# A plan's costs for transfers and TensorE transposes, and its table of priorities, replaced in an attention and two-MoE kernel

## The chip, the cores and the metric

The kernel runs on one core of one Trainium2 chip. The metric is the device time of one execution in microseconds (us): the median of several runs. A profiled execution of its own gives the trace that is read here.

## The reference, cut to what matters

The program computes attention with a window of 32 keys (heads 0 to 3 plain, heads 4 to 7 with every fourth position), and puts its output through two feed-forward blocks.

```python
B, H, S, D = 4, 8, 576, 64
scores = where(mask[h], q @ k.T / sqrt(D), -1e9)        # mask: 32 positions back, plain or dilated by 4
x = (softmax(scores) @ v).transpose(0, 2, 1, 3).reshape(B, S, 512)

x_prev = shift_by_one_position(x)
xk = mu_k * x + (1 - mu_k) * x_prev                     # 512 wide
xr = mu_r * x + (1 - mu_r) * x_prev
kk = relu(xk @ w_k)                                     # w_k 512 x 1024
x = sigmoid(xr @ w_r) * (kk * kk @ w_v)                 # w_r 512 x 512, w_v 1024 x 512

h = relu(x @ w_in); u, vv = halves(h)                   # w_in 512 x 1024
vs = einsum('ts,bsd->btd', w_spatial, layernorm(vv)) + b_spatial
out = (u * vs) @ w_out                                  # w_out 512 x 512
```

## The kernel before, in words

Every product in float32 is made of matmuls on numbers split into a high and a low part (names that end in h and l, or chunk numbers that end in _0 and _1), three matmuls for one product: high by high, high by low, low by high. Batch 0 to 3 follow one another; each batch has two halves of 320 and 256 positions in the first feed-forward block.

The weights w_k, w_r and w_v come in chunks of 128 rows by 512 columns (CH), one transfer of 128x1024 32-bit words each, since a number of the input fills two words. `split_weight` turns a chunk into numbers: the chunk lands in one of four places of the tiles room2 and room3 (`raws`), ScalarE makes two passes over it (temps<-room and room<-room), VectorE joins them (SCALAR_TENSOR_TENSOR temps<-temps,room), and then `split` makes the high part (a CAST or copy, on ScalarE or on VectorE) and the low part (TENSOR_TENSOR, number minus high part, on GpSimd or on VectorE). A matmul of w_v can only use a chunk when these steps are done: the high part for two of three matmuls, the low part for the third. The chunks of w_v are called wv_0 to wv_7 here; all eight are needed before the first half of batch 0 can leave the first feed-forward block, because that product sums over all of them in PSUM (psM0 to psM2 are three banks of it, with 128 output columns each, and the fourth 128 columns follow).

q, k and v of batch 0 come with large packets and are transposed on TensorE (`nat_load`, `nat_turn`: tile `early`). For batches 1 to 3 q and k come as transfers of 32 partitions by 18 by 32 numbers (tiles ld0 for q and ld1 for k, four transfers for a pair of heads), and VectorE transposes them (STREAM_TRANSPOSE qT<-ld0 and kT<-ld1; qT0 to qT3 are the four pairs of heads of a batch, so qT2 of the lists below is the third pair of batch 1).

The order of all this is not written by hand. Each operation is handed to `plan.add` with a cost in nanoseconds for each engine that may do it, the tiles it reads and writes and a due place (`plan.at`). `Plan.schedule` is a list scheduler: it keeps a clock for each engine and one for the transfers, and gives an engine the operation of the least priority among those that are ready. `Plan.tuned` makes that priority from `plan.at` and from TUNE, a table with four numbers for each group of operations: an amount added to the due place, one that grows over the group, and two penalties that say on which engine (VectorE, GpSimd) the operation is to be done. `Plan.order` then emits the operations in the order in which the plan's clock starts them. Where that clock sees TensorE idle for over 60 ns within the first 100 us, it puts matmuls of constant ones into psT2, whose result nothing reads: they are called fillers here. All operations are recorded through one helper, so nearly every row of the profile names one line (L487 before), and each engine runs its list in the order of the program; SyncE's list issues the transfers. It is the costs that decide the order of the program, and nothing that happens on the chip changes that order.

The costs that the change touches are those of transfers (`packets(n, size)`, a number of packets of one size) and those of TensorE's transposes of batch 0's q and k (`cost` in `nat_turn`).

Of the kernel before, what the change touches and what calls it, by code (L numbers as in the profile page):

```python
# [18 lines left out]
P = 128  # L19
B, H, S, D = 4, 8, 576, 64  # L20
# [3 lines left out]
KW = 64  # L24
# [13 lines left out]
def blocks(dil):  # L38
# [42 lines left out]
    ('nat', 0, 0): {'nat': (-33297, -203175, 792, 22)},  # L81
    ('nat', 0, 1): {'nat': (-32659, 22041, 792, 22)},
    ('nat', 1, 0): {'nat': (7637, 8404, 792, 22)},
    ('nat', 1, 1): {'nat': (9118, 46120, 792, 22)},
    ('nat', 2, 0): {'nat': (8986, 575, 792, 22)},
    ('out', 0): {'egh': (-7825, -292309, 0, 22), 'egl': (-6900, -201749, 1500, -300), 'ot': (-6966, 43586, -200, 22), 'out': (-7904, -38401, 792, 22), 'psB': (-5245, 95606, 792, 22)},
    ('out', 1): {'egh': (-6755, 194871, -200, 22), 'egl': (431, 278583, 792, 22), 'ot': (-3397, 200705, 200, 22), 'out': (-8375, -303115, 792, 22), 'psB': (-4713, -8735, 792, 22)},
    ('out', 2): {'egh': (-6918, -189364, -200, 0), 'egl': (-7254, 130638, 1500, 22), 'ot': (-21670, -382079, -200, 22), 'out': (-6469, -41265, 792, 22), 'psB': (-4762, -131208, 792, 22)},
    ('out', 3): {'egh': (199, -44669, 1500, 22), 'egl': (-4229, -3541, 1500, 300), 'ot': (-7861, -252610, 0, 22), 'out': (-9732, 143992, 792, 22), 'psB': (-11359, 200912, 792, 22)},
# [18 lines left out]
    ('sc', 0, 1, 1): {'psM': (14681, -101153, 792, 22), 'psS': (-3189, -31328, 792, 22)},  # L108
# [2141 lines left out]
```

## Time and profile before

| what | value |
|---|---|
| median of 3 runs | 574.64 us (574.34 to 575.77) |
| profiled execution, device time | 575.85 us |
| its span, first to last instruction | 574.0 us |
| TensorE busy | 556.9 us, 97% of the span |
| VectorE, ScalarE, GpSimd busy | 67%, 45%, 22% of the span |
| transfers over the span | 43.09 MB in 96255 packets, 81536 of them under 512 B |

The profiled execution lies 1.85 us above its own span, and at the upper end of the three runs: 1.21 us above their median. Matmuls are pipelined, so that a TensorE that is counted as busy may still stand for part of the time before the next operand. The unit of the trace's clock column is the full TensorE clock, 1.00.

### The profile page before, as it was taken

What the parts mean: (1) busy time and instruction counts of PE and PEld (TensorE: products, weight loads), DVE (VectorE), ACT (ScalarE), POOL (GpSimd) and SP (SyncE); (2) the same over time, 40 slices, a digit from 0 to 9 for tenths busy, and PEclk for the clock granted to TensorE, in tenths of its full rate; (3) what the DMA queues carried; (4) which work ended last, traced back from release to release, by engine and by line L of the source; (5) the groups of instructions that cost most, each with busy time, mean ns of one, the idle gap of its engine ahead of it and who ended that gap; (6) DMA issues with size and microseconds to landing.
All of it is one profiled execution on the core that took longest, in us unless ns stands there. A gap on an engine that the chain in (4) does not pass through costs nothing.

```text
span 574.0 us, 13856 instructions
## 1 busy us (share of the span) xinstructions
PE 556.9 (97%) x5767; PEld 503.4 (88%) x5778; DVE 385.1 (67%) x830; ACT 259.1 (45%) x573; POOL 126.6 (22%) x151
## 2 busy tenths in 40 slices
PE   9989799999999999999999999999999999999997
PEld 5557677799999999999999999988979988998996
DVE  3887596857996958459926341489897656856870
ACT  2776873642652445656837142365453223303102
POOL 0123301931471000320100000024232403203040
PEclk9979899999999999999999999999999999999999
DMA  9999975268344041324300000122010020001002
GB/s 218 235 198 203 198 198 85 44 134 125 45 73 101 2 107 27 98 70 150 109 5 2 1 25 1 47 86 73 23 51 2 1 69 26 1 1 73 2 1 91
DMA packets 96255, 43.09 MB, mean 75 GB/s; under 512 B 81536, under 2 KB 89216, under 8 KB 96192
## 3 DMA queue, kind: packets, MB, share of 16 engines
q1 hardware_dynamic: 96192, 42.21, 33.2%
q8 instruction: 45, 0.74, 0.6%
q14 instruction: 18, 0.15, 0.1%
HBM read 37.47 MB, written 4.72 MB: 74 GB/s over the span
## 4 chain that ended last, share of the span: by engine, by line
PE 86%; DMA 5%; DVE 5%; ACT 3%; issue 1%; SPq 0%; DVEq 0%; ACTq 0%
PE psM L487 60%; PE psB L487 17%; PE psT L487 6%; PE psS L487 3%; DMA room<-in_moe_w_v_dram 2%; DMA room<-in_moe_w_r_dram 2%; DMA ld<-in_k_dram 1%; DVE xm L487 1%; ACT room L487 0%; ACT xh L487 0%; SPq L487 0%; DVE st L487 0%; DVE gl L487 0%; DVE vl L487 0%; DVE x2h L487 0%
## 5 line engine op out<-in xcount | busy, mean ns | idle before, releaser
L487 PE MATMUL psM<-xh,wk 128*128 128x288 f32 (+2 forms) x512 | 122.9, 331 | 0.1
L487 PE MATMUL psM<-sq_dt.float32r,wv 128*128 128x288 f32 (+2 forms) x768 | 113.9, 299 | 2.0 <-ACT x L487 1.8
L487 PEld LDWEIGHTS psM<-sq_dt.float32r,wv 128*128 128x128 f32 x768 | 104.9, 188 | 5.1 <-ACT x L487 3.1
L487 PEld LDWEIGHTS psM<-xh,wk 128*128 128x128 f32 x512 | 88.2, 191 | 6.6 <-DVE x L487 0.3
L487 PE MATMUL psM<-xh,wr 128*128 128x288 f32 (+2 forms) x256 | 64.1, 309 | 3.0 <-ACT kr L487 3.0
L487 PE MATMUL psM<-xl,wk 128*128 128x288 f32 x192 | 56.5, 294 | 0.0
L487 PEld LDWEIGHTS psM<-xh,wr 128*128 128x128 f32 x256 | 45.1, 191 | 4.6 <-ACT kr L487 3.6
L487 ACT ACTIVATE kr<-psM 128x288 f32<-128x288 f32 (+2 forms) x48 | 19.7, 410 | 52.6 <-PE psM L487 50.6
L487 POOL TENSOR_TENSOR sq_dt.float32r<-kr,sq_dt.float32r 128x288 fp32r<-128x288 f32 (+2 forms) x29 | 25.0, 863 | 73.0 <-ACT sq_dt.float32r L487 30.5
L487 PE MATMUL psB<-wi,x2h 128*128 128x512 f32 x128 | 40.5, 397 | 0.3 <-ACT vt L487 0.3
L487 PE MATMUL psB<-wo,gh 128*128 128x512 f32 (+1 forms) x136 | 40.1, 379 | 0.0
L487 DVE SCALAR_TENSOR_TENSOR x<-x,psM 128x288 f32<-128x288 f32 (+2 forms) x32 | 14.1, 447 | 35.9 <-PE psM L487 35.8
L487 PE MATMUL psM<-wsh,vl 128*128 128x288 f32 x128 | 37.9, 296 | 0.3 <-DVE vl L487 0.3
L487 PE MATMUL psM<-xl,wr 128*128 128x288 f32 (+2 forms) x128 | 38.1, 297 | 0.0
L487 PE MATMUL psM<-wsh,vh 128*128 128x288 f32 x128 | 37.9, 296 | 0.0
L487 PE MATMUL psM<-wsl,vh 128*128 128x288 f32 x128 | 37.7, 295 | 0.0
L487 PEld LDWEIGHTS psM<-xl,wk 128*128 128x128 f32 x192 | 36.1, 188 | 0.0
L487 DVE SCALAR_TENSOR_TENSOR xm<-x,mu,xm 128x288 f32<-128x288 f32 (+2 forms) x56 | 29.7, 544 | 5.5 <-ACT xm L487 5.1
L487 POOL TENSOR_TENSOR xl<-xm,xh 128x288 fp32r<-128x288 f32 (+2 forms) x21 | 18.6, 891 | 64.5 <-ACT xh L487 19.2
L487 POOL TENSOR_TENSOR pr<-pr,st 128x384 f32<-128x384 f32 (+2 forms) x22 | 19.8, 901 | 36.8 <-DVE st L487 36.0
L487 DVE TENSOR_TENSOR g<-psM,bb 128x288 f32<-128x288 f32 x32 | 14.5, 455 | 19.6 <-PE psM L487 15.8
L487 PEld LDWEIGHTS psB<-wi,x2h 128*128 128x128 f32 x128 | 23.0, 188 | 4.9 <-ACT vt L487 0.5
(186 smaller groups left out, 1239.2 us busy)
## 6 DMA issues: line engine op xcount, KB each, us to landing
vw<-in_v_dram SPq DMA_DIRECT2D x36, 128.0 KB, 3.1
room<-in_moe_w_k_dram SPq DMA_DIRECT2D x8, 512.0 KB, 7.1
room<-in_moe_w_v_dram SPq DMA_DIRECT2D x8, 512.0 KB, 9.4
raw<-in_moe_w_in_dram SPq DMA_DIRECT2D x8, 512.0 KB, 3.8
ld<-in_q_dram SPq DMA_DIRECT2D x48, 72.0 KB, 3.2
ld<-in_k_dram SPq DMA_DIRECT2D x48, 72.0 KB, 3.1
vw<-in_v_dram SPq DMA_DIRECT2D x8, 288.0 KB, 5.4
room<-in_moe_w_r_dram SPq DMA_DIRECT2D x4, 512.0 KB, 8.0
```

Of the source, the lines that this page charges most:

```text
L487: return self.tc.keep_in_program_order(getattr(self.engine, name)(*args, **kw))
```

## The change

It does two things. First, the plan's costs: a transfer now costs a fixed 120 ns beside its packets, some packet sizes have another price, the price of 1024 B depends on the number of partitions, and a transpose on TensorE costs 55 ns plus at least 62 ns for each instruction. Second, every number of TUNE is replaced (124 lines, of which two are shown). No operation is added to the plan or taken from it. What changes is the order on each engine, which of two engines does some of the operations (VectorE's instructions go from 832 to 839, ScalarE's from 575 to 574, GpSimd's from 156 to 150 in the lists of the program), and the number of fillers, from 72 to 82. Behind the change the helper's line is L491.

```diff
 TUNE = {
-    ('T', 1): {'gh': (-4593, -1893, -200, 22), 'gl': (-7630, 2950, -600, 800), 'u': (-5281, 6834, 400, 2000)},
...
-    ('ld', 1, 0): {'ld': (171779, 143711, 792, 22)},
...
+    ('T', 1): {'gh': (-9212, -22400, 792, 22), 'gl': (-2114, -6089, 792, 2000), 'u': (-4045, 5784, 792, 2000)},
...
+    ('ld', 1, 0): {'ld': (204421, 176230, 792, 22)},
...
-def packets(n, size):
-
-    took = {128: 12.5, 256: 25, 512: 32, 896: 52, 1024: 58, 2048: 110, 2304: 125, 4096: 200}
-    return n * took[size] / 16
+def packets(n, size, rows=P):
+
+    took = {128: 12.5, 256: 23, 512: 34, 896: 50, 1024: 52 if rows == P else 76, 2048: 110, 2304: 125, 4096: 207}
+    return 120 + n * took[size] / 16
+
+
+def turns(k, n):
+    return 55 + k * max(62, 2 + 0.84 * n)
...
-                    packets(4 * n, 256), nat(x, i, 0)[0].rearrange("p (h d) -> p h d", d=D),
+                    packets(4 * n, 256) * 0.75, nat(x, i, 0)[0].rearrange("p (h d) -> p h d", d=D),
...
-                    packets(4 * o.shape[0], 1024) * (1 if t else 0.85), o.rearrange("p (h d) -> p h d", h=4),
+                    packets(4 * o.shape[0], 1024, 64 if t else P), o.rearrange("p (h d) -> p h d", h=4),
...
-            cost, ins = 0.43 * w, 4 * len(its)
+            cost, ins = turns(4 * len(its) // 2, w / (2 * len(its))), 4 * len(its)
...
-            cost, ins = len(its) * (30 + 0.4 * n), 2 * len(its)
+            cost, ins = turns(len(its), n), 2 * len(its)
...
-                        packets(nh * KW, 256 * n), vo[e * KW : (e + 1) * KW, :, g : g + n].rearrange("p h g d -> p h (g d)"),
+                        packets(nh * KW, 256 * n, KW), vo[e * KW : (e + 1) * KW, :, g : g + n].rearrange("p h g d -> p h (g d)"),
...
-                        packets(4 * P, 1024) * 0.85, vo[:, :, :4].rearrange("p h g d -> p h (g d)"),
+                        packets(4 * P, 1024), vo[:, :, :4].rearrange("p h g d -> p h (g d)"),
```

Three places of the order show what this does; they lie where the last chunks of w_v are loaded, split and used. In the names, a number at the end is the program's own of a tile, and "x3" after a row says that three such rows follow one another.

The first place is SyncE's list from the fifth chunk of w_v (wv_4) to the loads of q and k that follow the eighth. Before:

```order
L487 DMA room2_81<-in_moe_w_v_dram 128x1024
L487 DMA ld1_110<-in_k_dram 32x18x32
L487 DMA room3_82<-in_moe_w_v_dram 128x1024
L487 DMA room2_81<-in_moe_w_v_dram 128x1024
L487 DMA room3_82<-in_moe_w_v_dram 128x1024
L487 DMA ld1_110<-in_k_dram 32x18x32 x2
L487 DMA ld0_109<-in_q_dram 32x18x32 x4
L487 DMA ld1_110<-in_k_dram 32x18x32 x2
```


Only one load of k stands between the last four chunks here. With the change, from the same chunk on:

```order
L491 DMA room2_81<-in_moe_w_v_dram 128x1024
L491 DMA ld0_109<-in_q_dram 32x18x32
L491 DMA ld1_110<-in_k_dram 32x18x32 x2
L491 DMA room3_82<-in_moe_w_v_dram 128x1024
L491 DMA ld1_110<-in_k_dram 32x18x32 x2
L491 DMA room2_81<-in_moe_w_v_dram 128x1024
L491 DMA room3_82<-in_moe_w_v_dram 128x1024
L491 DMA ld0_109<-in_q_dram 32x18x32 x4
L491 DMA ld1_110<-in_k_dram 32x18x32 x4
```


The chunks are still in the order of w_v. The same 67 transfers stand ahead of the last of them in both programs; among them, transfers of q and k (ld0, ld1) have moved from ahead of the middle chunks to behind these, and the last chunk is followed by the q loads (ld0 x4) at once, which two loads of k preceded.

The second place is VectorE's list at the last two chunks, wv_6 and wv_7. Before:

```order
L487 SCALAR_TENSOR_TENSOR temps_83<-temps_83,room2_81 128x512
L487 TENSOR_TENSOR wv_5_0_1_1116<-temps_83,wv_5_0_0_1089 128x512
L487 SCALAR_TENSOR_TENSOR temps_83<-temps_83,room3_82 128x512
L487 TENSOR_TENSOR wv_6_0_1_1135<-temps_83,wv_6_0_0_1126 128x512
L487 TENSOR_TENSOR wv_7_0_1_1141<-temps_83,wv_7_0_0_1137 128x512
L487 STREAM_TRANSPOSE qT2_115<-ld0_109 128x144x4
L487 SCALAR_TENSOR_TENSOR x0_120<-x0_120,psM1_92 128x256
```


Here the two subtractions of wv_6 and wv_7 follow each other, with no cast between. With the change:

```order
L491 SCALAR_TENSOR_TENSOR temps_83<-temps_83,room2_81 128x512
L491 CAST wv_6_0_0_1126<-temps_83 128x512
L491 TENSOR_TENSOR wv_6_0_1_1131<-temps_83,wv_6_0_0_1126 128x512
L491 SCALAR_TENSOR_TENSOR temps_83<-temps_83,room3_82 128x512
L491 CAST wv_7_0_0_1145<-temps_83 128x512
L491 STREAM_TRANSPOSE qT2_115<-ld0_109 128x144x4
L491 TENSOR_TENSOR wv_7_0_1_1153<-temps_83,wv_7_0_0_1145 128x512
L491 STREAM_TRANSPOSE kT2_116<-ld1_110 128x144x4
L491 SCALAR_TENSOR_TENSOR x0_120<-x0_120,psM0_91 128x256
```


The casts to the high parts of wv_6 and wv_7 were on ScalarE and are now on VectorE, and the transposition of q of the next batch, which followed the last subtraction of w_v, now stands between that chunk's cast and its subtraction. From the last subtraction of w_r (wr_3_0_1) to that of w_v (wv_7_0_1) VectorE's list has 47 rows, where it had 35: the additions are five subtractions sq<-kr,sq of 128x256, four casts of w_v, three subtractions xl<-xm,xh, the transposition, and one TENSOR_SCALAR more of 128x320; one TENSOR_SCALAR and one CAST of 128x256 have left it.

The third place is TensorE's list where these chunks are used. Before:

```order
L487 LDWEIGHTS const-bfloat16-1.0
L487 MATMUL psT2_119<-const-bfloat16-1.0 128x512
L487 LDWEIGHTS const-bfloat16-1.0
L487 MATMUL psT2_119<-const-bfloat16-1.0 128x512
L487 MATMUL psM2_100<-sq_dt.float32r_738,wv_6_0_0_1126 128x256 x2
L487 MATMUL psM2_100<-sq_dt.float32r_738,wv_6_0_1_1135 128x256
L487 MATMUL psM1_92<-sq_dt.float32r_738,wv_6_0_0_1126 128x256 x2
L487 MATMUL psM1_92<-sq_dt.float32r_738,wv_6_0_1_1135 128x256
...
L487 MATMUL psM0_91<-sq_dt.float32r_738,wv_6_0_0_1126 128x256 x2
L487 MATMUL psM0_91<-sq_dt.float32r_738,wv_6_0_1_1135 128x256
L487 MATMUL psM0_91<-sq_dt.float32r_738,wv_7_0_0_1137 128x256 x2
...
L487 MATMUL psM1_92<-xh2_0_595,wk_0_0_2_225 128x320
```


Here the chain of wv_6 and wv_7 runs without a filler, up to the matmuls of w_k. With the change:

```order
L491 MATMUL psM2_100<-sq_dt.float32r_779,wv_6_0_0_1126 128x256 x2
L491 MATMUL psM2_100<-sq_dt.float32r_779,wv_6_0_1_1131 128x256
...
L491 MATMUL psM0_91<-sq_dt.float32r_779,wv_6_0_0_1126 128x256 x2
L491 MATMUL psM0_91<-sq_dt.float32r_779,wv_6_0_1_1131 128x256
L491 LDWEIGHTS const-bfloat16-1.0
L491 MATMUL psT2_119<-const-bfloat16-1.0 128x512
...
L491 MATMUL psM2_100<-sq_dt.float32r_779,wv_7_0_0_1145 128x256 x2
L491 MATMUL psM2_100<-sq_dt.float32r_779,wv_7_0_1_1153 128x256
...
L491 MATMUL psM0_91<-sq_dt.float32r_779,wv_7_0_0_1145 128x256 x2
L491 MATMUL psM0_91<-sq_dt.float32r_779,wv_7_0_1_1153 128x256
L491 LDWEIGHTS const-bfloat16-1.0
L491 MATMUL psT2_119<-const-bfloat16-1.0 128x512
...
L491 MATMUL psM0_91<-sq_dt.float32r_779,wv_0_0_0_913 128x256 x2
```


Before, two fillers stood ahead of the matmuls of wv_6 and none between wv_6 and wv_7, and the last bank's (psM0) matmuls of wv_6 came behind the first two banks' matmuls of wv_7. Now all nine matmuls of wv_6 stand ahead of wv_7's, seven fillers lie between them, and three follow behind. In all, 79 fillers stand ahead of wv_7's first matmul (72 before) and 63 matmuls of w_v (60 before).

From the 340th microsecond of the trace on, the lists of TensorE, ScalarE and VectorE are nearly the same in both programs.

## Rows read from the trace of the kernel before

**Rows 1.** The page, part 1: busy time, share, instructions of each engine.

```profile
PE 556.9 (97%) x5767; PEld 503.4 (88%) x5778; DVE 385.1 (67%) x830; ACT 259.1 (45%) x573; POOL 126.6 (22%) x151
```

**Rows 2.** Busy time by stretch; after the engines: granted clock, DMA share, GB/s.

```profile
0.00:86.00 86.00, 75.87 (x938) 55.03 (x950) 60.85 (x131) 56.96 (x121) 17.72 (x32) 0.94 1.04 209
86.00:570.00 484.00, 480.24 (x4826) 447.75 (x4825) 324.22 (x700) 201.73 (x451) 108.84 (x119) 1.00 0.22 51
570.00:574.00 4.00, 0.79 (x7) 0.59 (x5) 0.00 (x0) 0.38 (x1) 0.00 (x0) 0.91 0.21 73
```

**Rows 3.** DMA queues, 0 to 82 us: digits in 40 slices, packets.

```profile
DMA  0979999999999999999999999999999999969998
...
DMA packets 30404, 17.64 MB, mean 215 GB/s; under 512 B 25018, under 2 KB 27834, under 8 KB 30394
```

**Rows 4.** Timeline of SyncE, transfers' issue: start, length, row.

```profile
72.94 2.41 SPq L487 DMA_DIRECT2D room<-in_moe_w_v_dram  x3
...
78.96 3.56 SPq L487 DMA_DIRECT2D ld<-in_q_dram  x4
```

**Rows 5.** Timeline of ScalarE; in brackets the idle time before and its releaser.

```profile
79.20 0.67 ACT L487 ACTIVATE temps<-room 128x512 f32<-128x512 f32 x1 [1.92 <-DMA room<-in_moe_w_v_dram]
...
82.30 0.68 ACT L487 ACTIVATE temps<-room 128x512 f32<-128x512 f32 x1 [0.21 <-DMA room<-in_moe_w_v_dram]
82.88 0.66 ACT L487 ACTIVATE room<-room 128x512 uint32<-128x512 uint32 x1
```

**Rows 6.** Timeline of VectorE.

```profile
81.67 0.42 DVE L487 CAST wv<-temps 128x512 fp32r<-128x512 f32 x1
82.12 0.69 DVE L487 SCALAR_TENSOR_TENSOR temps<-temps,room 128x512 uint32<-128x512 uint32 x1
82.73 0.69 DVE L487 TENSOR_TENSOR wv<-temps,wv 128x512 fp32r<-128x512 f32 x1
83.57 0.70 DVE L487 SCALAR_TENSOR_TENSOR temps<-temps,room 128x512 uint32<-128x512 uint32 x1 [0.16 <-ACT room L487]
84.18 1.47 DVE L487 TENSOR_TENSOR wv<-temps,wv 128x512 fp32r<-128x512 f32 x2
85.56 1.20 DVE L487 STREAM_TRANSPOSE qT<-ld 128x576 f32<-128x576 f32 x1
86.61 1.06 DVE L487 SCALAR_TENSOR_TENSOR x<-x,psM 128x256 f32<-128x256 f32 x3
```

**Rows 7.** Timeline of TensorE's matmuls.

```profile
78.96 2.57 PE L487 MATMUL psT<-const-bfloat16-1.0 128*128 128x512 bf16 x11
...
84.66 2.49 PE L487 MATMUL psM<-sq_dt.float32r,wv 128*128 128x256 f32 x18
```

**Rows 8.** Waits of TensorE, whole run: total us, times, longest.

```profile
PE psM L487 <- ACT kr L487: 3.0, 1, 3.0
PE psM L487 <- issue: 2.6, 2, 2.4
PE psM L487 <- ACT x L487: 1.8, 4, 0.9
PE psM L487 <- ACT u L487: 1.3, 1, 1.3
...
PE psM L487 <- DVE x2l L487: 0.9, 1, 0.9
```

**Rows 9.** VectorE's groups by shape, 0 to 90 us: busy us, mean ns.

```profile
L487 DVE TENSOR_TENSOR pr<-psM,st 128x256 f32<-128x256 f32 x3 | 1.2, 403 | 1.2 <-PE psT L487 1.2
...
L487 DVE TENSOR_TENSOR xl<-xm,xh 128x320 fp32r<-128x320 f32 x1 | 0.5, 493 | 0.1
```

**Rows 10.** Busy time of three stretches ahead of 86 us.

```profile
34.00:38.00 4.00, 3.28 (x83) 2.65 (x84) 3.85 (x9) 2.12 (x7) 2.48 (x4) 0.50 1.02 207
60.40:65.10 4.70, 4.68 (x21) 4.27 (x21) 1.71 (x4) 3.09 (x8) 2.33 (x4) 0.64 1.19 184
59.50:85.60 26.10, 24.03 (x143) 19.34 (x146) 20.10 (x37) 20.50 (x42) 6.04 (x9) 0.93 0.96 202
```

More of the change, by code (lines that the diff above doesn't have):

```diff
@@ L57 @@
 TUNE = {
[23 rows of a table removed]
[L81 to L87, printed above, removed]
@@ L88 @@
-    ('out', 2): {'egh': (-6918, -189364, -200, 0), 'egl': (-7254, 130638, 1500, 22), 'ot': (-21670, -382079, -200, 22), 'out': (-6469, -41265, 792, 22), 'psB': (-4762, -131208, 792, 22)},
-    ('out', 3): {'egh': (199, -44669, 1500, 22), 'egl': (-4229, -3541, 1500, 300), 'ot': (-7861, -252610, 0, 22), 'out': (-9732, 143992, 792, 22), 'psB': (-11359, 200912, 792, 22)},
[18 rows of a table removed]
-    ('sc', 0, 1, 1): {'psM': (14681, -101153, 792, 22), 'psS': (-3189, -31328, 792, 22)},
[17 rows of a table removed]
-    ('start',): {'ident': (5981, -36163, 792, 22), 'identb': (6250, 262350, 792, 22), 'mask': (-30168, 206224, 400, 2000), 'xok': (-3545, 6792, 792, 22)},
[12 rows of a table removed]
@@ L139 @@
-    ('val', 0, 0, 0): {'psT': (20397, -228485, 792, 22), 'x': (3688, -173899, -600, 22)},
-    ('val', 0, 0, 1): {'psT': (9134, -31224, 792, 22), 'x': (2798, 154705, 200, 22)},
-    ('val', 0, 1, 0): {'psT': (9089, -79888, 792, 22), 'x': (5575, 67932, 400, 22)},
-    ('val', 0, 1, 1): {'psT': (19123, -128265, 792, 22), 'x': (8667, 35526, 1500, 22)},
-    ('val', 1, 0): {'psT': (1150, -93422, 792, 22), 'x': (6051, 20925, -200, 22)},
-    ('val', 1, 1): {'psT': (5213, 132263, 792, 22), 'x': (5217, -100910, -200, 22)},
@@ L145 @@
-    ('val', 2, 0): {'psT': (2089, 164082, 792, 22), 'x': (-4693, 128378, 1500, 22)},
-    ('val', 2, 1): {'psT': (20099, -298100, 792, 22), 'x': (7349, 170474, -200, 22)},
-    ('val', 3, 0): {'psT': (8358, -110270, 792, 22), 'x': (-188, 8721, 0, 22)},
-    ('val', 3, 1): {'psT': (1179, 21753, 792, 22), 'x': (3405, -256612, 400, 22)},
[26 rows of a table removed]
-    ('ws',): {'bb': (6918, -201337, 792, 22), 'psB': (-3510, 27307, 792, 22), 'raw2': (-3536, 31233, 792, 22), 'wsh': (-5305, 47701, 0, 22), 'wsl': (-7521, 576102, 792, 22), 'wslz': (3855, -137810, 792, 22), 'wst': (-5560, 2864, 792, 22)},
[6 rows of a table removed]
[23 rows of a table added]
@@ new lines @@
+    ('nat', 0, 0): {'nat': (3418, -160001, 792, 22)},
+    ('nat', 0, 1): {'nat': (7076, 15524, 792, 22)},
+    ('nat', 1, 0): {'nat': (8888, 3264, 792, 22)},
+    ('nat', 1, 1): {'nat': (11898, 25430, 792, 22)},
+    ('nat', 2, 0): {'nat': (7522, 3693, 792, 22)},
+    ('out', 0): {'egh': (-11529, -290843, 0, 800), 'egl': (-5870, -184165, 400, 2000), 'ot': (-6322, 32817, 200, 22), 'out': (-4463, -49224, 792, 22), 'psB': (-8954, 89293, 792, 22)},
+    ('out', 1): {'egh': (-9297, 163282, -200, 800), 'egl': (-3462, 268147, -600, -800), 'ot': (-2065, 215982, 0, 22), 'out': (-7165, -307258, 792, 22), 'psB': (-7345, -14808, 792, 22)},
@@ new lines @@
+    ('out', 2): {'egh': (-14523, -191998, -600, -800), 'egl': (-10553, 121440, 400, 2000), 'ot': (-6299, -366779, 1500, 22), 'out': (-13677, -57112, 792, 22), 'psB': (-10495, -135910, 792, 22)},
+    ('out', 3): {'egh': (-9913, -50100, 792, 800), 'egl': (-13558, 1950, -600, -300), 'ot': (-8415, -255843, 200, 22), 'out': (-7163, 133367, 792, 22), 'psB': (-11175, 178756, 792, 22)},
[18 rows of a table added]
+    ('sc', 0, 1, 1): {'psM': (-40, -122126, 792, 22), 'psS': (7865, -93583, 792, 22)},
[17 rows of a table added]
+    ('start',): {'ident': (6769, -55818, 792, 22), 'identb': (5249, 276562, 792, 22), 'mask': (5036, 211595, 400, 2000), 'xok': (6036, -15727, 792, 22)},
[12 rows of a table added]
@@ new lines @@
+    ('val', 0, 0, 0): {'psT': (5430, -212867, 792, 22), 'x': (2181, -181437, 400, 22)},
+    ('val', 0, 0, 1): {'psT': (10535, -31230, 792, 22), 'x': (6551, 179474, -600, 22)},
+    ('val', 0, 1, 0): {'psT': (7341, -92542, 792, 22), 'x': (4361, 94738, 200, 22)},
+    ('val', 0, 1, 1): {'psT': (5936, -132062, 792, 22), 'x': (-3073, 38617, 792, 22)},
+    ('val', 1, 0): {'psT': (-1669, -109657, 792, 22), 'x': (5722, 25960, 792, 22)},
+    ('val', 1, 1): {'psT': (-902, 96994, 792, 22), 'x': (-534, -55633, 400, 22)},
@@ new lines @@
+    ('val', 2, 0): {'psT': (-3932, 161697, 792, 22), 'x': (-1898, 134772, 1500, 22)},
+    ('val', 2, 1): {'psT': (5619, -304335, 792, 22), 'x': (682, 158024, -600, 22)},
+    ('val', 3, 0): {'psT': (18, -121171, 792, 22), 'x': (16859, -2077, -200, 22)},
+    ('val', 3, 1): {'psT': (4278, 29597, 792, 22), 'x': (2272, -226282, -200, 22)},
[26 rows of a table added]
+    ('ws',): {'bb': (-5847, -190127, 792, 22), 'psB': (499, 21932, 792, 22), 'raw2': (-4534, 72116, 792, 22), 'wsh': (-785, 46160, -200, 22), 'wsl': (-802, 584251, 792, 22), 'wslz': (-6583, -132294, 792, 22), 'wst': (-3177, 14606, 792, 22)},
[6 rows of a table added]
```

200 rows, old and new, of the table TUNE are left out of this document.

## The prediction

> **What bounds the kernel now.** I read the busy time by stretch first. From 86 to 570 us TensorE is busy for 480.24 of 484 us at the full clock [rows 2], so 3.76 us are all that better order could take from it there; over the span it is busy for 97% [rows 1]. The last 4 us drain the output, with the same work in both programs. The first 86 us are another regime: the DMA engines are at nine tenths or more in nearly all slices to 82 us, 17.64 MB at 215 GB/s, most of it in packets under 512 B [rows 3], and TensorE's 75.87 us [rows 2] contain fillers, such as 11 in a row at 78.96 [rows 7]. So I looked for what ends that regime. SyncE issues its last three chunks of w_v from 72.94 on [rows 4], and ScalarE starts on the last one at 82.30, 0.21 us after it ran out of work, released by that transfer [rows 5]: some 7 us lie between issue and landing, so the transfers stand in a queue and SyncE is ahead of it. Then VectorE joins the words of the last chunk at 83.57, makes the low part as the second of two subtractions that end at 84.18 + 1.47 = 85.65, and only then turns to the q of the next batch [rows 6]. TensorE's 18 matmuls from 84.66 on [rows 7] need that low part at about their ninth. Behind it stands a fixed amount of TensorE work with nearly no gap. The end of the kernel therefore moves with the end of that subtraction, with the fillers that stand behind it, and with waits after 86 us.
>
> **The change part by part.** *Transfers.* The order puts the same 67 transfers ahead of the last chunk of w_v. A queue that is full lands the last one when their bytes are through, whatever their order, and SyncE has some 7 us in hand [rows 4, 5]. I take 0 for its landing. The trace doesn't show what mixing small and large packets otherwise does; a transfer of 72 KB (32 x 18 x 32 numbers, of four bytes) takes 0.34 us of the queue at 215 GB/s [rows 3], and I bound the landing by three such, 1.0 us to either side. Chunks in the middle land earlier: about 432 KB less (two loads of q, three of v) stand ahead of the last chunk of w_r, 2.0 us at 215 GB/s. That gives TensorE nothing while it still waits for wv_7, since all eight chunks go into one sum.
>
> *The last split, on VectorE.* I walk the new rows with the old row's times, from the join of wv_6 at 82.12 [rows 6], whose input lands as before. The join takes 0.69 and ends at 82.82 with the handover; the cast, formerly on ScalarE, takes 0.45 from its start to the next start (81.67 to 82.12): 83.27. The subtraction takes 0.61 from start to start (82.12 to 82.73): 83.88, where the join of wv_7 stood at 83.57; ScalarE's second pass of that chunk, at 82.88, ends at 83.54 [rows 5], so VectorE is now the later of the two. Join 0.70, 84.58; cast 0.42, 85.0; then the transposition of q, which is ahead of the subtraction now: 1.05 from start to start (85.56 to 86.61), 86.05; the subtraction 0.69, 86.74. Against 85.65 that is **+1.09**. Without the transposition it would be 85.0 + 0.69 = 85.69, so it is nearly the whole of this term. It needs four q loads that stand directly behind the last chunk on SyncE; they were issued from 78.96 on [rows 4], and now two loads of k fewer precede them. At 0.34 us each, four are down 1.4 us after the chunk, at about 83.5 to 84, and the start at 85.0 leaves them 1 us. That cover hides them; without it, each tenth that they are late is added.
>
> *TensorE behind the last split.* Three matmuls of wv_6 that came behind the low part of wv_7 are now ahead of it: 2.49 / 18 = 0.14 us each, **-0.41**. Three fillers stand behind wv_7 that weren't there, 2.57 / 11 = 0.23 us each [rows 7]: **+0.70**. The seven fillers between wv_6 and wv_7 are 1.6 us; the nine matmuls of wv_6 can run from about 83.3, so they and the fillers end at 83.3 + 1.3 + 1.6 = 86.2, ahead of 86.74: hidden by the wait for the subtraction, and if that came at 85.65 as before, 0.5 us of them would show.
>
> *Other costs of the plan* (transposes of batch 0, prices of packets, engines for splits) act through the order alone and so fall under these terms, or lie in the first 80 us, where the queue covers them, or behind 86 us, where the waits on x, u and x2l, 1.8, 1.3 and 0.9 us [rows 8], stand, the last two among rows that the order leaves nearly as they are. I take 0; the bound of a gain is 2.7 us, x and x2l gone, and that of a loss the same, those two doubled.
>
> *Fillers and the clock.* Before, TensorE waited for 2.4 and 3.0 us in single waits [rows 8], and behind each the granted clock was lower: 0.50 in 34 to 38 us, which is the lower of its two levels, 1.2 GHz, and 0.64 in 60.4 to 65.1, a mix of the two levels [rows 10]. The Trainium skill (TensorE: Matmul & The Clock Gate, "HAM oscillation — how this bites in real kernels") says the same of waiting for transfers: when the wait for the next operand is longer than the compute before it, the engine is throttled and the next tile starts cold. Here that speaks against a later low part, but seven fillers and nine matmuls run right ahead of the wait, which is then 86.74 - 86.2 = 0.5 us: I take no loss of clock.
>
> Sum: 1.09 - 0.41 + 0.70 = 1.38 us. On the profiled execution's own 575.85 that makes 577.2; that execution is 1.21 us above the median of the runs, 574.64, so the median goes to **576.0**. That is +0.24%, and a measurement of this kernel can tell about 0.3%, 1.7 us, from no change: 572.9 to 576.4 is "same".
>
> **The rivals.** *No change worth the name:* TensorE is fed the high parts of wv_7 and its later work without needing the low part so soon, or the transposition starts earlier because the whole list does. Then only the fillers and the three matmuls remain, +0.3, or nothing: 574.6 to 575.2. For it: ScalarE has two casts fewer. Against it: wv_6 lands when it did, and the join of wv_7 can't pass the one of wv_6.
>
> *Faster:* the mixing of packets lands the last chunk up to 1.0 us sooner, and the new order takes up to 2.7 us out of the waits on x and x2l. 576.0 - 1.0 - 2.7 = 572.3; with both only half, 574.2. For it: the two waits are the largest left. Against it: the surroundings of x2l hardly move in the order.
>
> *Slower, VectorE becomes the bound between w_r and w_v:* without the transposition, which is counted, it gets five subtractions of 128x256 at 0.40, four casts at 0.45, three subtractions xl at 0.4 to 0.5 [rows 6, 9] and a little that cancels, 4.8 us, in 59.5 to 85.6 where it was idle for 26.10 - 20.10 = 6.0 us [rows 10]. If that idle time can be used, it costs nothing. If it stays idle because each join still waits for its own chunk, only the 2.0 us by which the w_r chunk is earlier are left: 4.8 - 2.0 = 2.8 us late, 576.0 + 2.8 = 578.8. It decides from the point where the join of wv_6 starts behind 82.12.
>
> *Slower, the clock:* if the fillers end well before the low part comes (a late q load would do it), the wait grows to the length at which rows before show a lower clock. Over 4.7 us at a mean of 0.64 [rows 10] about 1.7 us of work are lost, 4.7 x 0.36: 576.0 + 1.7 = 577.7. By the Trainium skill's section just named, this is what a wait for data does as a rule; the trace agrees with it for its two long waits [rows 8, 10].
>
> **How the numbers follow.** The sum 0.42 (its own range 575.2 to 576.9, from half the landing's bound; 0.12 of it lies above 576.4); no change 0.12; faster 0.20; VectorE 0.14; clock 0.12. Predicted is the sum, 576.0. The range leaves out half of the faster case's lower end and the top of VectorE's: 572.2 to 578.6. Same: 0.30 + 0.12 = 0.42. Slower: 0.12 + 0.14 + 0.12 = 0.38. Faster: 0.20.
>
> **What would show it.** Right: ScalarE's first pass of the last chunk of w_v starts at 82 to 82.6 after a wait for its transfer; VectorE has a row of q's transposition ahead of the last subtraction, which ends at 86.5 to 87; TensorE's fillers, then matmuls of w_v at their end, three fillers, and behind 86 us again about 480 of 484 us busy. Wrong: the transfer row moves by over 1 us (the queue isn't what I took it for); VectorE has no idle time in the 5 us before the last join (it has become the bound); the granted clock falls below 1.00 at 84 to 92 us; or the waits on x, u and x2l grow or go.

## The result, and the profile after

| what | before | after |
|---|---|---|
| median, 20 runs of each in turn | 574.74 us | 577.74 us |
| lowest and highest | 571.32 to 577.46 | 575.32 to 580.45 |
| profiled execution, device time | 575.85 us | 577.19 us |
| its span | 574.0 us | 575.4 us |

The ratio is 1.0055, with a 95% interval of 1.0037 to 1.0074: the changed kernel is 3.0 us slower (2.1 to 4.3). Forecast were 576.0 us in a range of 572.2 to 578.6, and "no change that can be told" as the likeliest sign. The two profiled executions lie 1.34 us apart, so these traces can account for that much, and the rest of the 3.0 us lies in executions without a trace. A second traced execution of each came later: 574.52 us before and 575.07 after, 0.55 us apart.

Busy time by stretch, after; the first two rows answer to [rows 2], the fourth to [rows 10]:

```profile
0.00:86.00 86.00, 78.99 (x966) 55.44 (x967) 65.74 (x146) 55.91 (x120) 9.04 (x20) 0.94 0.94 213
86.00:570.00 484.00, 478.18 (x4808) 444.77 (x4806) 316.77 (x692) 198.89 (x450) 118.60 (x125) 1.00 0.21 50
...
20.00:40.00 20.00, 16.06 (x384) 10.11 (x382) 18.23 (x48) 16.33 (x35) 1.25 (x3) 0.89 1.11 278
59.50:85.60 26.10, 25.59 (x170) 20.12 (x169) 23.87 (x47) 17.05 (x37) 0.32 (x3) 1.00 0.76 170
60.00:80.00 20.00, 19.49 (x130) 15.36 (x129) 19.69 (x41) 16.55 (x36) 0.11 (x1) 1.00 0.89 201
340.00:400.00 60.00, 56.91 (x374) 52.42 (x373) 32.97 (x80) 24.03 (x53) 7.51 (x9) 1.00 0.14 41
```

The same view of the kernel before, for three stretches that were not shown:

```profile
20.00:40.00 20.00, 16.19 (x337) 11.72 (x334) 17.02 (x47) 16.40 (x34) 4.71 (x6) 0.85 1.08 229
60.00:80.00 20.00, 18.47 (x108) 15.13 (x111) 15.22 (x28) 15.55 (x35) 5.34 (x7) 0.91 1.03 230
...
340.00:400.00 60.00, 58.57 (x387) 54.26 (x387) 34.26 (x84) 25.44 (x55) 9.17 (x11) 1.00 0.17 48
```

Three things are to be seen. From 86 to 570 us TensorE's busy time fell by 2.06 us, and 1.66 of them lie in 340 to 400. From 60 to 80 us VectorE went from 15.22 to 19.69 of 20 us: it is full. And from 20 to 40 us the DMA engines moved 278 GB/s where they had moved 229, at nearly the same busy share.

SyncE's list, and ScalarE's two first passes of the last two chunks of w_v, after:

```profile
69.26 2.98 SPq L491 DMA_DIRECT2D room<-in_moe_w_v_dram  x2
```

```profile
75.08 0.66 ACT L491 ACTIVATE temps<-room 128x512 f32<-128x512 f32 x1
...
76.19 0.66 ACT L491 ACTIVATE temps<-room 128x512 f32<-128x512 f32 x1
```

The last chunk landed at 75.5 us, by its transfer's row, where it had landed at 82.2. ScalarE no longer waits for it: there is no bracket as in [rows 5]. VectorE and TensorE, where [rows 6] and [rows 7] stood:

```profile
78.44 0.68 DVE L491 SCALAR_TENSOR_TENSOR temps<-temps,room 128x512 uint32<-128x512 uint32 x1
79.16 0.43 DVE L491 CAST wv<-temps 128x512 fp32r<-128x512 f32 x1
79.61 0.69 DVE L491 TENSOR_TENSOR wv<-temps,wv 128x512 fp32r<-128x512 f32 x1
80.22 0.68 DVE L491 SCALAR_TENSOR_TENSOR temps<-temps,room 128x512 uint32<-128x512 uint32 x1
80.94 0.43 DVE L491 CAST wv<-temps 128x512 fp32r<-128x512 f32 x1
81.28 1.16 DVE L491 STREAM_TRANSPOSE qT<-ld 128x576 f32<-128x576 f32 x1
82.30 0.67 DVE L491 TENSOR_TENSOR wv<-temps,wv 128x512 fp32r<-128x512 f32 x1
```

```profile
83.03 1.70 PE L491 MATMUL psT<-const-bfloat16-1.0 128*128 128x512 bf16 x7
84.38 1.42 PE L491 MATMUL psM<-sq_dt.float32r,wv 128*128 128x256 f32 x9
85.64 0.83 PE L491 MATMUL psT<-const-bfloat16-1.0 128*128 128x512 bf16 x3
86.31 0.62 PE L491 MATMUL psM<-sq_dt.float32r,wv 128*128 128x256 f32 x3
```

The last subtraction ends at 82.97, 2.68 us ahead of before's 85.65. TensorE then runs seven fillers that nothing covers, and three more: the gain is nearly spent. The first matmul of the second block (x2h by wi) starts at 357.39, where it started at 357.75; in the second traces it is 357.21 after and 356.45 before, so which kernel is ahead there changes from trace to trace. From there to the last matmul 214.7 us pass, against 213.05. TensorE's waits, whole run, as in [rows 8]:

```profile
PE psT L491 <- ACT x L491: 2.0, 2, 1.3
PE psM L491 <- DVE vl L491: 1.8, 2, 1.0
PE psT L491 <- DVE pr L491: 1.8, 1, 1.8
PE psM L491 <- ACT u L491: 1.3, 1, 1.3
...
PE psM L491 <- DVE x2l L491: 0.9, 1, 0.9
```

The waits on u and x2l stand as they were. The two largest new ones, on x and on pr (into psT), lie in the first 45 us. A wait on vl (low part of the layer norm's output), 0.3 us before, is 1.8 now, and it lies at 390 to 392 us.

### The profile page after: what moved, and what is told of

Read it like the earlier page. It is cut to its first block, busy times and chain, and to the rows that moved or that the text cites. A ratio compares the mean times of both kernels' runs of the same rounds, so it can differ in the third digit from the quotient of the medians.

```text
span 575.4 us, 13888 instructions
## 1 busy us (share of the span) xinstructions
PE 559.3 (97%) x5788; PEld 502.1 (87%) x5788; DVE 382.5 (66%) x837; ACT 255.6 (44%) x572; POOL 127.6 (22%) x145
## 4 chain that ended last, share of the span: by engine, by line
PE 86%; DVE 6%; ACT 3%; SPq 2%; issue 1%; DMA 1%; POOL 0%; DVEq 0%; ACTq 0%; POOLq 0%
PE psM L491 62%; PE psB L491 16%; PE psT L491 7%; SPq L491 2%; PE psS L491 2%; DVE st L491 1%; DVE wk L491 1%; DMA vw<-in_v_dram 1%; DVE pr L491 1%; DVE x2h L491 1%; DVE vl L491 0%; ACT room L491 0%; ACT xm L491 0%; ACT xh L491 0%; ACT wk L491 0%
## 5 line engine op out<-in xcount | busy, mean ns | idle before, releaser
L491 PE MATMUL psM<-xh,wk 128*128 128x288 f32 (+2 forms) x512 | 121.1, 330 | 1.0 <-ACT kr L491 1.0
L491 PE MATMUL psM<-sq_dt.float32r,wv 128*128 128x288 f32 (+2 forms) x768 | 112.7, 298 | 0.2 <-ACT x L491 0.2
L491 PEld LDWEIGHTS psM<-sq_dt.float32r,wv 128*128 128x128 f32 x768 | 104.7, 188 | 2.6 <-ACT x L491 0.7
L491 PEld LDWEIGHTS psM<-xh,wk 128*128 128x128 f32 x512 | 87.5, 190 | 7.4 <-ACT kr L491 1.3
L491 PE MATMUL psM<-xh,wr 128*128 128x288 f32 (+2 forms) x256 | 62.1, 303 | 0.7 <-DVE kr L491 0.3
L491 PE MATMUL psM<-xl,wk 128*128 128x288 f32 x192 | 56.5, 294 | 0.0
L491 ACT ACTIVATE kr<-psM 128x288 f32<-128x288 f32 (+2 forms) x50 | 20.4, 408 | 63.4 <-PE psM L491 62.3
L491 POOL TENSOR_TENSOR x2l<-x,x2h 128x288 fp32r<-128x288 f32 x23 | 18.9, 842 | 132.9 <-DVE x2h L491 74.9
L491 PEld LDWEIGHTS psM<-xh,wr 128*128 128x128 f32 x256 | 44.3, 188 | 2.9 <-DVE kr L491 0.8
L491 DVE SCALAR_TENSOR_TENSOR x<-x,psM 128x288 f32<-128x288 f32 (+2 forms) x32 | 14.3, 451 | 40.7 <-PE psM L491 40.7
L491 POOL TENSOR_TENSOR pr<-pr,st 128x384 f32<-128x384 f32 (+2 forms) x27 | 25.5, 949 | 70.3 <-DVE st L491 55.7
L491 PE MATMUL psB<-wi,x2h 128*128 128x512 f32 x128 | 40.3, 396 | 0.0
L491 PE MATMUL psB<-wo,gh 128*128 128x512 f32 (+1 forms) x136 | 40.2, 379 | 0.0
L491 PE MATMUL psM<-wsh,vl 128*128 128x288 f32 x128 | 37.8, 296 | 1.8 <-DVE vl L491 1.8
L491 PE MATMUL psM<-wsh,vh 128*128 128x288 f32 x128 | 37.9, 296 | 0.0
L491 PE MATMUL psM<-wsl,vh 128*128 128x288 f32 x128 | 37.7, 294 | 0.0
L491 DVE SCALAR_TENSOR_TENSOR xm<-x,mu,xm 128x288 f32<-128x288 f32 (+2 forms) x56 | 29.9, 539 | 11.7 <-ACT xm L491 11.3
L491 PE MATMUL psM<-xl,wr 128*128 128x288 f32 (+2 forms) x128 | 37.6, 294 | 0.0
L491 PEld LDWEIGHTS psM<-xl,wk 128*128 128x128 f32 x192 | 36.1, 188 | 0.0
L491 ACT ACTIVATE xm<-x,rest 128x288 f32<-128x288 f32 (+2 forms) x42 | 22.0, 533 | 20.1 <-DVE x L491 7.6
L491 POOL TENSOR_TENSOR sq_dt.float32r<-kr,sq_dt.float32r 128x288 fp32r<-128x288 f32 (+1 forms) x28 | 23.5, 839 | 32.9 <-ACT sq_dt.float32r L491 29.7
L491 POOL TENSOR_TENSOR xl<-xm,xh 128x288 fp32r<-128x288 f32 x21 | 17.3, 829 | 46.5 <-DVE xh L491 22.5
```

The lines of the kernel that those rows point to most:

```text
L491: return self.tc.keep_in_program_order(getattr(self.engine, name)(*args, **kw))
```

## The experiments

All ratios are against the kernel before, run in turn on the same chip. In the edits, `op` finds an operation of the plan by its group and key, and `behind(i, j)` moves i in the finished list to the place right behind j.

**The late table of before in the changed kernel.** If the loss sits in the late order, the late groups' old numbers should bring it back.

```diff
-    ('T', 1): {'gh': (-9212, -22400, 792, 22), 'gl': (-2114, -6089, 792, 2000), 'u': (-4045, 5784, 792, 2000)},
+    ('T', 1): {'gh': (-4593, -1893, -200, 22), 'gl': (-7630, 2950, -600, 800), 'u': (-5281, 6834, 400, 2000)},
...
```

The groups T, out, sp, u, vt, x2, ws, ws4, p2, (w, wi) and (w, wo), and the loads of w_in and w_out, take before's numbers.

> The changed kernel with the numbers of TUNE of the kernel before for the groups of the second feed-forward block alone (w_in, w_spatial and w_out, x2, vt, u, sp, T, out); all rows up to about 340 us are those of the changed kernel. Theory (the loss has two parts, and one of them is the new order of the second block, where TensorE waits 1.04 and 0.76 us for vl at 390 and 392 us and the trace falls back by 1.7 us between 357 and 560 us): 1.7 us faster than the changed kernel, so 1.3 us above the kernel before, ratio 1.002. Rival (the loss is made in the first 90 us, and the rest moves with it): no gain, ratio 1.005.

Measured: 578.88 us, 1.0066 [1.0043, 1.0089]. Nothing came back, as the rival had it, but this doesn't place the loss in the first 90 us: the wait on vl fell to 0.7 us, and others stand in its place:

```profile
PE psB L491 <- DVE wsl L491: 1.4, 1, 1.4
...
PE psM L491 <- DVE vl L491: 0.7, 1, 0.7
PE psM L491 <- DVE u L491: 0.6, 1, 0.6
```

From the first x2h by wi to the end it took 214.9 us. **The reverse,** the changed kernel's late numbers in the kernel before:

> The reverse: the kernel before with the changed numbers of TUNE for the second feed-forward block alone; the first 340 us are those of the kernel before. Theory of two parts: 1.7 us slower than the kernel before, ratio 1.003, with waits for vl at about 390 us. Rival (all of it is made in the first 90 us): ratio 1.000.

Measured: 592.57 us, 1.0301 [1.027, 1.0332], with 6.1 us of waiting for vh and 3.5 for u:

```profile
PE psM L487 <- ACT vh L487: 6.1, 1, 6.1
PE psM L487 <- ACT u L487: 3.5, 2, 3.0
```

So the table's parts can't be exchanged: its numbers fit the plan that they stand in. To test one place, the finished list has to be edited, not the table.

**The whole halves of the change.** The new costs with the old table, then the old costs with the new table (the edit is one half of the diff, the cost functions with their calls or TUNE):

> The first half of the change alone: the new costs of transfers and transposes, with the old table TUNE. Theory (the numbers of the table fit only the plan with which they were found, as the swap of the second block's numbers showed, which cost 18 us): slower than both kernels, by 1% or more against the one before. Rival (the costs matter little, and the table makes the order): within 0.3% of the kernel before.

> The second half alone: the new table TUNE with the old costs. Theory: slower than both kernels, by 1% or more against the one before. Rival (the table makes the order): within 0.3% of the changed kernel, ratio 1.0055.

Measured: 595.31 us, 1.0377 [1.0349, 1.0405], and 607.1 us, 1.0567 [1.0525, 1.061]. Each half alone is far worse than both. The cost of the change can't be split between them.

**The two low parts vl earlier,** in the finished list, so that they stand ahead of the casts of x2h:

```diff
+        behind(op(("vt", 0), ("vl", 0)), op(("vt", 0), ("mv", 0)))
+        behind(op(("vt", 0), ("vl", 1)), op(("vt", 0), ("vh", 1)))
```

> The changed kernel, planned as it is, with two rows of VectorE's list put elsewhere behind the plan: the subtraction that makes vl of the first 128 positions stands right behind the statistics of the second 128 (it followed ten rows later, though its vh is ready at 385.7 us in the trace), and that of the second 128 right behind its own vh. Theory (the loss of 1.7 us between 357 us and the end is TensorE's wait for vl, 1.04 and 0.76 us, which are late by VectorE's order alone): the two waits go to 0.3 us or less in all, 1.4 us or more are gained from 357 us to the end (213.3 us there, the changed kernel 214.7, the kernel before 213.0), ratio 1.003. Rival (what stands in front of vl now, casts of x2h and the next statistics, is late in its turn, or TensorE waits elsewhere): 214.5 us or more in that stretch, ratio 1.005.

Measured: 576.77 us, 1.0037 [1.0013, 1.0061]; the wait on vl is 0.2 us and the stretch to the end 213.46. The trace bears the theory out in the main (1.2 us of 214.7 gained, where it asked for 1.4 or more); the median lies 1.0 us below the changed kernel's 577.74, which the two intervals can't tell from none.

**The kernels before and after once more,** without an edit, for a second trace of each:

> The kernel before, not changed, for a second trace of it and for the width of the measurement. Ratio 1.000. If the queue of transfers runs the same in every execution, the last chunk of w_v lands at 82.2 us again, within 1 us; if its speed changes from execution to execution, it lands several us elsewhere, and the time moves by less than that.

> The changed kernel once more, for a second trace and for the measurement. Ratio 1.0055 within its interval (1.0037 to 1.0074). If VectorE's list sets the stage of w_v, its subtractions take 19.3 us from the first to the last again, whenever the chunks land; the stretch from the first matmul of the second block to the end takes 214.7 us.

Measured: 574.52 us, 0.9983 [0.9964, 1.0003], and 578.36 us, 1.0082 [1.005, 1.0115]. The last chunk landed at 80.8 us in the first, 1.4 us earlier than before; in the second the chain of subtractions took 19.3 us again. The traced execution of the second was the fastest of its eight, 575.07 us, and its stretch to the end is 212.81 us, as short as before's. What differs is this. VectorE at that place in the first trace of the changed kernel:

```profile
387.97 0.95 DVE L491 CAST x2h<-x 128x288 fp32r<-128x288 f32 x1
388.84 1.27 DVE L491 TENSOR_TENSOR vl<-vt,vh 128x512 fp32r<-128x512 f32 x1
390.04 0.80 DVE L491 CAST x2h<-x 128x288 fp32r<-128x288 f32 x1
390.75 1.18 DVE L491 TENSOR_TENSOR vl<-vt,vh 128x512 fp32r<-128x512 f32 x1
```

GpSimd beside it:

```profile
387.95 4.54 POOL L491 TENSOR_TENSOR x2l<-x,x2h 128x288 fp32r<-128x288 f32 x5 [0.88 <-PE psB L491]
```

VectorE in the second trace of the same kernel:

```profile
387.93 0.30 DVE L491 CAST x2h<-x 128x288 fp32r<-128x288 f32 x1
388.15 0.68 DVE L491 TENSOR_TENSOR vl<-vt,vh 128x512 fp32r<-128x512 f32 x1
388.75 0.30 DVE L491 CAST x2h<-x 128x288 fp32r<-128x288 f32 x1
388.97 0.68 DVE L491 TENSOR_TENSOR vl<-vt,vh 128x512 fp32r<-128x512 f32 x1
```

GpSimd beside it:

```profile
388.10 5.30 POOL L491 TENSOR_TENSOR x2l<-x,x2h 128x288 fp32r<-128x288 f32 x5 [1.27 <-ACT x2h L491]
```

The rows are the same, in the same order. Where GpSimd's subtraction starts 0.02 us ahead of VectorE's cast, VectorE's rows take 1.7 to 3.2 times as long. Where VectorE starts first, its rows keep their length and GpSimd's five take 0.76 us longer. But the first start alone isn't a rule that these traces bear out. In the kernel before a cast is slow although VectorE's row ahead of it had begun before GpSimd's:

```profile
389.21 0.68 DVE L487 TENSOR_TENSOR vl<-vt,vh 128x512 fp32r<-128x512 f32 x1
389.44 2.38 POOL L487 TENSOR_TENSOR x2l<-x,x2h 128x288 fp32r<-128x288 f32 x3 [0.92 <-DVE x2h L487]
389.82 0.80 DVE L487 CAST x2h<-x 128x288 fp32r<-128x288 f32 x1
```

The low part vl of the first 128 positions took 1.29 us there as well (at 387.78, beside GpSimd), and TensorE waited 0.3 us for it: long rows at this place are not new with the change. The wait on vl was there in four of the five traces with this order and missing in this one.

**Fifteen fillers less** in front of and among the w_v matmuls:

```diff
...
-                            res.append((None, room[0]))
+                            fills += 1
+                            if fills <= 67:
+                                res.append((None, room[0]))
```

> The changed kernel without its last 15 fillers: the five ahead of the matmuls of wv_6, the seven ahead of those of wv_7 and the three behind. Theory (in the changed kernel the last chunk of w_v lands at 75.5 us, its split is done at 82.97, and from 76 us on it is TensorE's own list, fillers included, that sets the time): the matmuls of wv_7 end at about 83.9 instead of 85.7, and with the three fillers behind it 2.4 us are gained, ratio to the kernel before about 1.001. Rival (the split of the chunks or the queue still sets the end, as the prediction had it): at most the three fillers, 0.7 us, ratio 1.004. A second rival (a TensorE without fillers loses its clock): a granted clock below 1.00 between 80 and 90 us and no gain, or a loss.

Measured: 577.54 us, 1.0036 [1.0014, 1.0059]. The first x2h by wi starts at 356.88, 0.5 us earlier, not 2.4. Even that can't be told from none: four traces that keep all the fillers and the changed kernel's order up to there have it at 356.63 to 357.39. Without the fillers TensorE waits for VectorE:

```profile
83.45 1.09 PE L493 MATMUL psM<-sq_dt.float32r,wv 128*128 128x256 f32 x7 [0.71 <-DVE wv L493]
85.06 0.62 PE L493 MATMUL psM<-sq_dt.float32r,wv 128*128 128x256 f32 x3 [0.51 <-DVE x L493]
```

The chunk landed at 79.1 here, 3.6 us later than in the changed kernel's trace, and still there are 19.3 us from the start of the first w_v subtraction to the start of the last, as in both traces of the changed kernel. So the landing doesn't set the end of the split; VectorE's list does.

**The transposition of q behind the last split as well:**

```diff
+        behind(op(("qk", 1, 1), ("qT", 2, 0)), op(("w", "wv"), (("wv", 7, 0), 1)))
```

> The changed kernel without its last 15 fillers, as before, and with the transposition of q (qT2) put right behind the last subtraction of w_v. The prediction's own term: that subtraction ends 1.05 us earlier, at about 82.3 instead of 83.4 us in the run without the fillers, TensorE's matmuls of wv_7 follow it, ratio 1.0036 - 0.0018 = 1.002. Rival (the chain of VectorE ahead of it is what is late, and the transposition only fills a wait): the same end, ratio 1.0036.

Measured: 578.15 us, 1.0064 [1.0035, 1.0092], neither of the two ratios. The 19.3 us became 18.4, so the transposition's 1.0 us in this chain was real. But two transpositions now stand ahead of the row x<-x,psM, and TensorE waits for that instead:

```profile
85.32 0.63 PE L503 MATMUL psM<-sq_dt.float32r,wv 128*128 128x256 f32 x3 [1.22 <-DVE x L503]
```

**Nine subtractions moved to GpSimd,** with the fifteen fillers less:

```diff
...
+            if e == "dve" and ops[i][6][0][0] in ("kl", "xl") and "pool" in ops[i][0]:
+                res[k] = (i, "pool")
```

> The changed kernel without its last 15 fillers, with nine subtractions (five sq<-kr,sq, four xl<-xm,xh) that stand in VectorE's list between the last split of w_r and that of w_v given to GpSimd, at the same places of the program. Theory (VectorE is the bound from w_r to w_v in the changed kernel: it is busy for 9.9 and 9.8 of 10 us from 60 to 80 us, and its last subtraction of w_v ends at 82.3 to 83.4 us whether the last chunk lands at 75.5, 78.1 or 79.1): 5 x 0.40 + 4 x 0.45 = 3.8 us of its work go, the last subtraction ends 1.5 to 3 us earlier, and the time falls by 1 us or more, ratio 1.001 or less. Rival (GpSimd takes twice as long for each and slows VectorE while it runs, so TensorE waits for the squares instead): no gain, ratio 1.004 or more.

Measured: 578.24 us, 1.0075 [1.0049, 1.0101]; the chain of subtractions became longer, 20.0 us. VectorE was busy for 17.20 us of 60 to 80, but two of its rows that took 0.69 and 0.55 us in the changed kernel took 1.6 and 2.1 times as long beside GpSimd:

```profile
68.44 1.11 DVE L508 TENSOR_TENSOR wv<-temps,wv 128x512 fp32r<-128x512 f32 x1
...
71.37 1.14 DVE L508 SCALAR_TENSOR_TENSOR xh<-x,mu,xh 128x320 f32<-128x320 f32 x1
```

A 128x256 subtraction took 0.42 us on VectorE in the changed kernel and 0.80 on GpSimd here. The Trainium skill (GPSIMD Engine Reference, "4.1 Engine selection") says that GpSimd is about twice as slow for two inputs; the trace agrees.

**All of these edits in one:**

> The four edits together: 15 fillers less, q's transposition behind the last subtraction of w_v, nine subtractions on GpSimd, vl early. If the parts add up: 1.0036 - 0.002 - 0.002 - 0.0025 = 0.997, about 1.6 us below the kernel before. If the front parts hide one another (the last chunk's landing takes over as the bound, at 75 to 79 us plus 3.4 us for its split): 0.999.

Measured: 578.02 us, 1.007 [1.0042, 1.0097]; neither sum held. The end is short (213.46 us), the front late: the first x2h by wi at 359.45.

**The third pair's transpositions and eight loads put further back,** behind the operation g of the group (v, 0, 0), with the fillers less and vl early:

```diff
+        j = op(("v", 0, 0), ("g", 0, 2, 0))
+        q_, k_ = op(("qk", 1, 1), ("qT", 2, 0)), op(("qk", 1, 1), ("kT", 2, 0))
+        for i in (q_, k_, *range(k_ + 1, k_ + 9)):
+            behind(i, j)
+            j = i
```

> The changed kernel without its last 15 fillers, with vl early as before, and with the transpositions qT2 and kT2 (and the eight loads that follow them) put behind the three rows x<-x,psM that free TensorE's banks, instead of ahead of the last subtraction of w_v and ahead of those rows. Theory (in the run with only qT2 moved the subtraction ended earlier, but kT2 and qT2 then stood ahead of x<-x,psM and TensorE waited 1.22 us for it): the last subtraction ends at about 82.4 us, the wait for x at 85 us goes, the first matmul of the second block comes 1.2 us or more earlier than in the run without the fillers (356.9), at 355.7 or less, and with the 1.3 us of vl the ratio is 1.000. Rival (qT3 and kT3 and their loads are then late, and TensorE waits for them behind 90 us): 356.9 or more, ratio 1.0035.

Measured: 580.82 us, 1.0112 [1.0079, 1.0144], and the first x2h by wi starts at 361.95, not at 355.7 or less. VectorE then waits for the loads of the fourth pair, and the row x<-x,psM behind them is late for TensorE:

```profile
92.66 1.15 DVE L509 STREAM_TRANSPOSE qT<-ld 128x576 f32<-128x576 f32 x1 [4.21 <-DMA ld<-in_q_dram]
93.67 0.39 DVE L509 SCALAR_TENSOR_TENSOR x<-x,psM 128x256 f32<-128x256 f32 x1
...
94.12 1.15 PE L509 MATMUL psM<-xh,wk 128*128 128x320 f32 x2 [2.56 <-DVE x L509]
```

No version beat the kernel before.

## Why the range held and some of its steps did not

The median lies inside the range, 1.7 us above the forecast, and on the side that had 0.38 where "no change" had 0.42. The forecast for the profiled execution, 577.2, met the measured 577.19 by luck: its sum put +1.38 us into the first stage and 0 behind it, and these two executions show -0.36 and +1.65. The second pair shows +0.76 and -0.2. So what the range caught was the size of the sum, and not the mechanism. The sum's own range was narrowly off too: half the landing's bound gives 575.5 to 576.5, not 575.2 to 576.9.

**The landing: wrong.** The step "a queue that is full lands the last one when their bytes are through, whatever their order", with 1.0 us to either side, failed. The chunk landed at 75.5 and 75.6 us in two traces of the changed kernel, at 82.2 and 80.8 in two of the kernel before. An earlier issue doesn't explain it: in the second trace of the kernel before SyncE issued this chunk at 71.4 us, ahead of the changed kernel's 71.9, and it took 9.4 us to land where the other took 3.6. In the runs with an edit of the changed kernel it landed at 75 to 80 us, so one kernel's landing varies by several us as well. The queue of the changed kernel up to the landing, as in [rows 3]:

```profile
DMA  0898996899999999999999998799999999999866
...
DMA packets 28365, 17.38 MB, mean 230 GB/s; under 512 B 22979, under 2 KB 25795, under 8 KB 28355
```

Nearly the same bytes went through, 17.38 and 17.64 MB, at 230 and 215 GB/s. Before, 2,039 more packets under 512 B had gone by then (25018 - 22979). At 576 packets for a load of 72 KB (128 B each) these are 3.5 loads more from behind the chunk in the list than with the change (an estimate from the packet counts, since the same 67 transfers stand ahead), so what stands behind it takes its share too. Counted in packets the rates lie nearer together: 371 per us before and 376 after, and 378 and 391 in the second traces. No run changed the mixture of packets alone, and what sets the rate stays open.

**The last split: its length right, its start wrong.** From the join of wv_6 to the end of the last subtraction the walk gave 4.62 us; 78.44 to 82.97 is 4.53. The transposition was to cost 1.05 and takes 1.02 (81.28 to 82.30). But the walk began at 82.12, the old row's time of that join, and the new rows began at 78.44, where VectorE's list got there. The rival "VectorE becomes the bound between w_r and w_v" has the right mechanism: 19.69 of 20 us busy, a chain of 19.3 us whether the chunk lands at 75.5 or 79.1. Its price of 2.8 us wasn't paid, since the list began earlier; so the term of +1.09 for the end of the split came out at -2.68.

**Fillers: partly right.** Seven were to be hidden by the wait for the low part. The low part was ready at 82.97, and they start at 83.03: nothing hid them. Three behind take 0.67 (85.64 to 86.31), forecast 0.70, but the sum counted them in full, and most of them lie over a wait: the next matmuls need the row x<-x,psM, which starts at 85.84, and without the fillers TensorE waited 0.51 us for it. Taking fifteen away gave back 0.5 us in the trace at most, since VectorE's lateness stands right under them. With the split earlier and the fillers bare, the front came out 0.36 us ahead in the first pair of traces and 0.76 behind in the second, where the sum had 1.38 behind.

**Other waits: the value 0 wrong, the bound met.** The prediction read the wait on x, 1.8 us, as one behind 86 us; only 0.9 of it lies there, so the bound should have been 1.8 and not 2.7. That 0.9 went and a wait of 1.0 on kr came; x2l and u stayed, as argued. The new wait is on vl, 1.5 us more than before, in an execution in which GpSimd's subtractions start just ahead of VectorE's casts and low parts. The two traces of one kernel show how it comes and goes, and the edit of two places in the list takes it away; that GpSimd's start makes it is read from rows that overlap, and no run changed that alone here. Between the first two traces 1.65 us more from the first x2h by wi to the end, less 0.36 in front, leaves 1.29 of the 1.34 us between the profiled executions.

**The clock: right where it was forecast, and open elsewhere.** The granted clock at 80 to 90 us is 1.00 in the changed kernel's trace. Earlier it falls in both kernels: in the changed one, where TensorE had waited 1.8 us for pr and 1.3 us for x, to 0.50 in parts of these two stretches:

```profile
28.00:34.00 6.00, 5.13 (x95) 2.80 (x96) 5.73 (x15) 4.45 (x11) 0.00 (x0) 0.72 1.08 261
38.00:46.00 8.00, 6.74 (x104) 5.22 (x102) 6.26 (x16) 5.49 (x13) 1.10 (x1) 0.57 1.06 240
```

The second trace of the kernel before has no such fall, behind a wait of 2.0 us:

```profile
0.00:86.00 86.00, 75.51 (x959) 52.38 (x960) 62.32 (x134) 57.16 (x121) 17.67 (x32) 1.00 1.00 209
```

It reaches the first x2h by wi 1.3 us ahead of the first trace of the same kernel, whose clock in this stretch was 0.94.

**What stays open.** The medians lie 3.0 us apart, the profiled executions 1.34, and the fastest execution of the changed kernel that was traced (575.07 us) has no loss at vl at all. Some 1.7 us of the median lie in executions that no trace shows. The wait on vl, which comes and goes, is a candidate: the ratio without it is 1.0037, against 1.0055 and 1.0082 with it, which is 1.0 to 2.6 us, and the intervals overlap. The clock is another: the mean granted clock is 0.994 over 73 executions of the kernel before and 0.992 over 28 of the changed one, and among the first 20 of these it is 0.993 for the faster ten and 0.990 for the slower ten. A fall of 0.002 is worth about 1.2 us of 575 (an estimate, which takes TensorE's work as what sets the time throughout). No run held the clock or the early waits apart from the order, so what the 3.0 us are made of is not shown.

## What to carry to other kernels

When a planner's list replaces another, walk each engine's list for its own sum before asking when its inputs land: here VectorE went from 76% to 98% busy over 20 us, and the landing no longer mattered. Numbers tuned on one plan held for that plan alone here: the costs or the priorities table put in by itself lost 3.8% and 5.7%. To test a cause in such a kernel, move single rows of the finished list, and take a second trace of the same kernel before trusting a difference of 1 us.

## What the runs showed of the hardware that was not expected

Rows of VectorE and of GpSimd that overlap can be longer on one of the two engines, and which one pays can change between executions: a cast of 128x288 took 0.30 or 0.95 us and a subtraction of 128x512 0.68 or 1.27 on VectorE, and GpSimd's five rows 5.30 or 4.54, in two executions of one kernel whose starts differ by some 0.1 us. The DMA engines moved 229 or 278 GB/s in the same 20 us at a busy share of 1.08 and 1.11 (242 and 283 at 1.04 and 1.06 in the second traces): the kernels differ there in the order of the transfers, but no run changed that alone.
